# The fifth row block of x^T phi(k) by seven 64-column products, right ahead of KV

## The chip, the core and the metric

The kernel runs on one core of a Trainium2 chip. The metric is the time of one execution on the device in microseconds (us); the kernel before takes 182.53 us, the median of 3 runs from 182.36 to 182.84.

## What is computed

x is 2048 x 640 in bf16, and two linear-attention blocks A and B with their own weights read the same x. For each of them, with H = 32 heads of 20 columns:

```python
qkv = (x @ wqkv).reshape(B, S, 3, H, Dh)          # q, k, v
phi = lambda t: where(t > 0, t + 1, exp(t)) + 1e-6
pq, pk = phi(q), phi(k)
kv  = einsum("bhsd,bhse->bhde", pk, v)            # per head, 20 x 20
z   = einsum("bhsd->bhd", pk)
num = einsum("bhqd,bhde->bhqe", pq, kv)
den = einsum("bhqd,bhd->bhq", pq, z) + 1e-6
block = (num / den) @ wo
```

The output is g·A(x) + (1 − g)·B(x), where g = sigmoid((x · gate_w) summed over the columns), one number for each row.

## The kernel before

No v is ever computed. As kv = phi(k)^T x wv, the kernel makes G = x^T phi(k) (640 x 640, in two halves of 320 columns, `GT[0]` and `GT[1]`, called lo and hi here) and then KV = G^T wv for each head's group of columns. KV is folded into wo (M = KV·wo, 640 x 640), so that the last stage is (phi(q)/den)·M for A and B together.

**Order of the work.** The whole program is a hand-written order; each engine works through its own list in that order, and waits on semaphores where its data or its buffer isn't ready. The stages are: k and q of A (16 row chunks, then column units), A's G stage (`g_all(0)`), k of B (16 chunks of ten 320-column products, `k_chunk`, L227) with A's KV and M in between, q of B in ten units (`q_pass`), B's G stage, and then the pairs (`Pair`, L600), which make the output rows two blocks at a time with shared partial products. phi of a chunk is an exp on ScalarE (L205), a clamp on VectorE (L210) and a maximum on VectorE: either straight from the bank (L214) or, for a "lifted" chunk, from a copy with 1 added that ScalarE makes (L209, then L212).

**The G stage.** G is 5 row blocks of 128. `g_pass` (L307) makes the fifth one, columns 512 to 640 of x, by 32 products of 320 columns (`g_mm`, L328); in its course `z_pass` (L438) makes the sums of phi(k) from rows that VectorE added before (`z_sum`, `z_half`, `z_last`), and `zsel` from them. The other four blocks are made by `g_strassen` (L375): a 2 x 2 scheme with seven products on blocks of x (256 columns by 1024 rows) and of phi(k) (320 columns by 1024 rows), each of 16 matmuls (`g_prod`, L366). Its sums of x are `x_sum(1)` to `x_sum(4)` (SX1 to SX4, L334), those of phi(k) `k_sum(b, 1)` to `k_sum(b, 4)` (TK, L345), all on VectorE through `add_rows` (L546). The partial products lie in two PSUM slots called even and odd and are added on VectorE (L387, L435) with copies p1, u2 and u3 in SBUF.

Inside this stage stands den (`rec_pass`, L516; `by_group`, L172): 40 products of 256 columns by 32 rows of output, four side by side on the array. Behind it `rec(h)` on VectorE multiplies by the gate's factor (d, L525), takes the reciprocal (L530) and sends the result through DRAM (`r_store`, `r_load`) to R, by which `scale` (L576, L579) multiplies phi(q) in place.

**KV and M.** `kv_mm` (L457) takes six groups of columns times five row blocks, two tiles of 60 or 40 rows side by side: 60 products. `kv_mask` cuts the heads out. For A it stands behind k chunk 1 of B (`kv_a`, L480), for B behind the first pair's p1. `m_a` (L505) folds A's wo in between the later k chunks, `m_b` (L784) B's at the start of the pairs, with the copies from PSUM shared by ScalarE and VectorE (L791) and a round trip through DRAM (`m_store`, `m_load`). `load_wo` brings wo into a buffer with the tag "wo".

**Sums for the pairs.** `p_diff` (L550) and `p_sums` (L555) make differences and sums of phi(q) of A and B in four parts of 256 columns on VectorE; part 0 of one of them is given to GpSimd (L799). `m_sum` makes those of M; `TM[0]` of A's M is made in B's G stage.

**Queues.** SyncE (SP) issues most DMAs in program order; ScalarE issues some of r_load, the load of wq for B and a few stores.

Of the kernel before, what the change touches and what calls it, by code (L numbers as in the profile page):

```python
# [24 lines left out]
NW = 6  # L25
# [7 lines left out]
def kernel(  # L33
# [21 lines left out]
    psum = banks.enter_context(tc.tile_pool(name="psum", bufs=1, space=bass.MemoryType.PSUM))  # L55

    turn = [0]

    def ps_raw(name, slot=None):

        if slot is None:
            slot = turn[0]
            turn[0] = (slot + 1) % 4
        return psum.tile([P, 4 * HB], BF16, tag=f"ps{slot}", name=name)
# [9 lines left out]
    GT2 = persist.tile([P, 2 * DT, HF], BF16, name="GT")  # L74
    GT = [GT2[:, n * DT:(n + 1) * DT, :] for n in range(2)]
# [19 lines left out]
    SX[4] = flat(M[1], "p c d -> p (c d)", ic)  # L95
    TK = [{k: flat(pqT[1], "p c s -> p (c s)", HF, k - 1) for k in (1, 2, 3, 4)}, {}]
# [4 lines left out]
    early = persist.tile([P, hc * HF], BF16, name="TM0")  # L101
    TM = [early[:, 0:DT * HF].rearrange("p (c n) -> p c n", c=DT)] + [None] * 3
    TK[1][2] = early[:].rearrange("p (i n) -> p i n", i=hc)
# [60 lines left out]
    for n in (HB,) * 6 + (HB // 2,):  # L164
        nc.tensor.matmul(warm[:, 1, 0:n], lhsT=one_l, rhs=one_r[:, 0:n], start=True, stop=True)
# [141 lines left out]
    def g_pass(b, c, slot):  # L307

        pt = ps(f"g{'AB'[b]}", slot)
        for i in range(ST):  # L310
            if b == 0 and i == 4:
                gate_exp()
            if i == (8 if b else 13):
                zsel = z_pass(b)
                if b:
                    p_diff(part[0])
                else:
                    x_sum(2)
                    gate_done(0)
            if b == 1 and i == 13:  # L320
                p_diff(part[1])
            for hf in range(2):
                g_mm(c, i, hf, pt)
        for hf in range(2):
            nc.scalar.copy(out=GT[hf][:, c, :], in_=pt[:, hf, 0:HF])
        return zsel

    def g_mm(c, i, hf, pt):  # L328
        nc.tensor.matmul(  # L329
            pt[:, hf, 0:HF], lhsT=xn[:, i, c * P:(c + 1) * P], rhs=pk[:, i, hf * HF:(hf + 1) * HF],  # L330
            start=(i == 0), stop=(i == ST - 1),
        )

    def x_sum(k, cuts=(0, hc)):  # L334

        x11, x21 = [xn[:, 0:hc, n:n + ic] for n in (0, ic)]
        x12, x22 = [xn[:, hc:ST, n:n + ic] for n in (0, ic)]
        a, b, op = {
            1: (x21, x22, ALU.subtract), 2: (x11, SX[1], ALU.subtract),
            3: (x21, x11, ALU.subtract), 4: (x12, SX[2], ALU.subtract),  # L340
        }[k]
        for lo, hi in zip(cuts, cuts[1:]):
            add_rows(SX[k][:, lo:hi], a[:, lo:hi], b[:, lo:hi], op)
# [21 lines left out]

    def g_prod(pt, left, right, first, lo=0, hi=hc):  # L366

        for i in range(lo, hi):
            for n in range(2):
                nc.tensor.matmul(  # L370
                    pt[:, n, 0:HF], lhsT=left[:, i, n * P:(n + 1) * P], rhs=right[:, i, :],
                    start=(first and i == 0), stop=(i == hc - 1), skip_group_check=not first,
                )

    def g_strassen(b, den):  # L375

        x11, x12 = [xn[:, k:k + hc, 0:ic] for k in (0, hc)]
        x22 = xn[:, hc:ST, ic:2 * ic]
# [4 lines left out]
        def temp(name):  # L383
            return work.tile([P, 2, HF], FP32, tag="osb", name=name, bufs=3)

        def add(dst, pt, sb):
            nc.vector.tensor_tensor(out=dst, in0=pt[:, :, 0:HF], in1=sb[:], op=ALU.add)  # L387

        even, odd = ps("gs0", 0), ps("gs1", 1)
        g_prod(even, x11, b11, True, 0, 1 - b)  # L390
        rec = den()
        rec(0)
        g_prod(even, x11, b11, True, 1 - b)
        p1 = temp("p1")
        nc.scalar.copy(out=p1[:], in_=even[:, :, 0:HF])
        if b == 0:
            x_sum(3)
        else:
            rec(1)
        g_prod(odd, SX[2], TK[b][2], True)  # L400
        u2 = temp("u2")
        add(u2[:], odd, p1)
        if b == 0:
            x_sum(4)
        else:
            p_diff(part[2])
            p_diff(part[3])
            m_sum(0)
        g_prod(even, x12, b21, False)
        nc.scalar.copy(out=lo[:, 0:2, :], in_=even[:, :, 0:HF])  # L410
        if b == 0:
            rec(1)
        r_load(b, 1, nc.scalar)
        if b == 0:
            wq[1] = load_w(1, "q", nc.scalar)
        scale(b, 0, 2, 0)
        g_prod(odd, SX[3], TK[b][3], False)
        u3 = temp("u3")
        add(u3[:], odd, p1)
        scale(b, 2, 4, 0)  # L420
        even = ps("gs0", 0)
        g_prod(even, SX[1], TK[b][1], True)
        if b == 1:
            load_wo(1, nc.sync)
        add(hi[:, 2:4, :], even, u3)
        scale(*((b, 0, 2, 1) if b else (b, 4, 5, 0)))
        g_prod(odd, x22, TK[b][4], False)
        if b == 1:
            scale(1, 4, 5, 0)
        add(lo[:, 2:4, :], odd, p1)  # L430
        if b == 1:
            scale(1, 2, 4, 1)
        g_prod(even, SX[4], b22, False)
        for n in range(2):
            nc.vector.tensor_tensor(out=hi[:, n, :], in0=even[:, n, 0:HF], in1=u2[:, n], op=ALU.add)  # L435
        if b == 0:
            scale(0, 0, 2, 1)
    def z_pass(b):  # L438

        dst = ps(f"z{'AB'[b]}", 1 - b)[:, 0, 0:DT * H]  # L440
# [16 lines left out]
    def kv_mm(b, dst):  # L457

        for k in range(NW):
            for i, c in enumerate((4, 2, 3, 0, 1)):  # L460
                for p0, hf, d0, w in kv_groups(k):
                    nc.tensor.matmul(
                        dst[p0:p0 + w, k * WT[0]:k * WT[0] + w], lhsT=wv[b][:, c, hf * HF + d0:hf * HF + d0 + w],
                        rhs=GT[hf][:, c, d0:d0 + w], start=(i == 0), stop=(i == DT - 1), tile_position=(0, p0),
                    )

# [12 lines left out]

    def kv_a():  # L480

        pt = ps("kvA")
        kv_mm(0, pt[:, 0])
        kv_mask(pt[:, 0])
# [31 lines left out]
    def rec_pass(b, zsel, slot):  # L516
# [5 lines left out]
        def rec(h):  # L522
# [8 lines left out]
            eng = nc.scalar if h else nc.sync  # L531
# [33 lines left out]

    def m_sum(k):

        lo, hi = slice(0, HF), slice(HF, D)
        a, b = M[0], M[1]
        left, right = {  # L570
            0: (a[:, :, hi], a[:, :, lo]), 1: (b[:, :, hi], TM[0]),
# [14 lines left out]
    def prod(dst, left, right, i, first):  # L586

        r0 = i * P
        for c in range(DT):
            nc.tensor.matmul(  # L590
                dst, lhsT=left[:, c, r0:r0 + P], rhs=right[:, c, :], start=(first and c == 0), stop=(c == DT - 1), skip_group_check=not first,
# [4 lines left out]

    def tmp(name, tag):
        return work.tile([P, HF], FP32, tag=tag, name=name)

    class Pair:  # L600

        def __init__(self, i):
            self.i = i
            self.last = i == ST // 2 - 1
            self.p1s, self.p15 = [xn[:, k * hc + i, :].bitcast(FP32) for k in range(2)]

        def store(self, k, lo=0, hi=D):
            eng = nc.scalar if self.last and (k or lo > HF) else nc.sync
# [36 lines left out]
        def p6(self):  # L645
            prod(self.at("x"), xT[:, :, 0:SH], TM[1], self.i, True)
            self.u6 = tmp("u6", "ex")
            nc.scalar.copy(out=self.u6[:], in_=self.at("x"))  # L648

        def u25(self):  # L650
            self.v = tmp("v", "zr")
            out_add(self.v[:], self.u6[:], self.p15)
# [23 lines left out]
    def load_w(b, which, eng, cuts=(0, DT)):  # L676
        lo = {"q": 0, "k": D, "v": 2 * D}[which]
        t = wpool.tile([P, DT, D], BF16, tag="w" + which, name=f"w{which}{'AB'[b]}")
# [3 lines left out]

    def load_wo(b, eng):
        t = wo_sb[b] = wpool.tile([P, NW, D], BF16, tag="wo", name=f"wo{'AB'[b]}")
# [28 lines left out]
    def g_all(b):  # L713

        zsel = g_pass(b, DT - 1, 2 - b)
        g_strassen(b, lambda: rec_pass(b, zsel, 3 - b))


# [3 lines left out]
    for n in range(2):  # L722
        for i in range(CB if n else 0, CB * 2 * n):
            k_chunk(0, i, lifted=i % 2 == 0)
        for m in (0, 2):
# [4 lines left out]
    wv[0] = load_w(0, "v", nc.sync)  # L730
    load_wo(0, nc.sync)
    wk[1] = load_w(1, "k", nc.sync)

# [6 lines left out]
    with tc.manual_schedule():  # L740
        for i in range(hc + 1, ST):
# [3 lines left out]
            if i == hc + 3:  # L745
                k_sum(0, 1)
# [4 lines left out]
        g_all(0)  # L751

        turn[0] = 3
        for i in range(ST):
            k_chunk(1, i, lifted=i in (5, 7, 9, 13))
            if i in (3, 5, 7):
                scale(0, i // 2 + 1, i // 2 + 2, 1)
            if i > 3 and i % 2 == 0:
                m_a(i // 2 - 2)
            if i == 1:  # L760
                kv_a()
                wv[1] = load_w(1, "v", nc.sync)
# [6 lines left out]
        g_all(1)  # L769
# [8 lines left out]
        with late_pool("mid") as mid:  # L778
# [15 lines left out]
            pairs[0].p1()  # L794
            scale(1, 4, 5, 1)
            kv = acc["z"][1]
            kv_mm(1, kv)
            kv_mask(kv)
            p_sums(slice(0, 2 * P), (1,), nc.gpsimd)  # L799
            pairs[1].p1()  # L800
# [92 lines left out]
```

## Time and profile before

| | |
|---|---|
| median of 3 runs | 182.53 us (182.36 to 182.84) |
| the profiled execution | 182.66 us |
| its span in the profile | 180.9 us (1.76 us lie outside) |
| granted TensorE clock | 1.000 |

In the profile PE is TensorE's products, PEld its weight loads, DVE VectorE, ACT ScalarE, POOL GpSimd and SP SyncE. The page's first part gives busy time, share of the span and number of instructions of each engine. A row of the chain of waits, in order of time, gives start, length, and what stood on the path. A row of a timeline gives start, length, engine, line, operation, the tiles (out<-in), their shapes, and in brackets the idle time of the engine ahead of it and what ended it. A row of the groups by line gives engine, operation, tiles, shapes and count, then the busy time in us, the mean of one in ns, and the idle time ahead. All starts count from the span's start.

### The profile page before, as it was taken

To read this page: it belongs to the slowest core of one execution; us is meant where nothing else is said; L and a number is where in the kernel's file an instruction comes from. 1 tells how busy PE (TensorE), PEld (TensorE's weight loads), DVE (VectorE), ACT (ScalarE), POOL (GpSimd) and SP (SyncE) were. 2 spreads that over 40 slices of the span, in tenths; PEclk is the share of its full clock that TensorE was granted. 3 is DMA by queue.
4 is the path that set the end of the run, shared out by engine and by line. 5 is a ranking of instruction groups with operands and counts; after the bars stand their busy time and mean duration, and the time that the engine had idled before them with its cause. 6 is when DMAs were issued, how large, how long until landed. Compare 5 with 4: busy or idle time off the path is not lost.

```text
span 180.9 us, 3415 instructions
## 1 busy us (share of the span) xinstructions
PE 176.8 (98%) x1340; PEld 119.3 (66%) x1345; DVE 147.6 (82%) x247; ACT 85.8 (47%) x140; POOL 5.4 (3%) x18
## 2 busy tenths in 40 slices
PE   8999999999999999999999999999999999999993
PEld 4565657765577777777775555577777777777772
DVE  0386868989999896888778999969999799977863
ACT  2245846889972101378784779931101763111010
POOL 6000000000000000000000000000002300000000
PEclk9999999999999999999999999999999999999999
DMA  5999999524100217331115000000325451133323
GB/s 183 214 261 170 240 364 297 110 38 145 58 0 5 72 32 226 91 127 35 57 34 186 23 0 0 0 0 18 112 79 144 129 179 60 36 109 112 109 92 127
DMA packets 22842, 19.33 MB, mean 107 GB/s; under 512 B 10538, under 2 KB 22058, under 8 KB 22826
## 3 DMA queue, kind: packets, MB, share of 16 engines
q1 hardware_dynamic: 20744, 16.95, 34.0%
q10 hardware_dynamic: 2082, 2.17, 3.7%
q8 instruction: 10, 0.16, 0.4%
q14 instruction: 6, 0.05, 0.1%
HBM read 12.29 MB, written 4.53 MB: 93 GB/s over the span
## 4 chain that ended last, share of the span: by engine, by line
PE 95%; DMA 2%; issue 0%; DVE 0%; ACTq 0%
PE gs L370 17%; PE kA L218 12%; PE ox L590 12%; PE kB L218 12%; PE qB L281 12%; PE qA L281 6%; PE oz L590 6%; PE qA L291 5%; PE gA L329 2%; PE gB L329 2%; DMA wkA<-in_A_wqkv_dram 2%; PE ow L590 2%; PE qA L301 1%; PE mA L494 1%; PE s L494 1%; PE oy L590 1%
## 5 line engine op out<-in xcount | busy, mean ns | idle before, releaser
L218 PEld LDWEIGHTS <-xT 128*128 128x128 bf16 x320 | 31.0, 98 | 13.1 <-DVE xT L243 0.8
L210 DVE TENSOR_SCALAR e<-e 128x640 bf16<-128x640 bf16 (+2 forms) x53 | 18.9, 357 | 7.2 <-ACT e L205 6.6
L218 PE MATMUL kA<-wkA,xT 128*128 128x320 bf16 (+1 forms) x160 | 22.8, 300 | 0.3 <-DMA wkA<-in_A_wqkv_dram 0.3
L218 PE MATMUL kB<-wkB,xT 128*128 128x320 bf16 x160 | 23.1, 299 | 0.0
L281 PE MATMUL qB<-xT,wqB 128*128 128x512 bf16 x98 | 21.6, 379 | 0.1
L205 ACT ACTIVATE e<-kB 128x640 bf16<-128x640 f32 x16 | 11.3, 704 | 15.8 <-DMA wqB<-in_B_wqkv_dram 9.4
L281 PEld LDWEIGHTS <-wqB 128*128 128x128 bf16 x100 | 11.7, 117 | 9.7
L205 ACT ACTIVATE e<-kA 128x640 bf16<-128x640 f32 x16 | 11.2, 705 | 8.4 <-PE kA L218 8.4
L205 ACT ACTIVATE e<-qA 128x1024 bf16<-128x1024 f32 (+1 forms) x11 | 10.4, 946 | 6.4 <-PE qA L291 5.1
L648 ACT COPY u<-ox 128x320 f32<-128x320 f32 x8 | 3.4, 426 | 20.4 <-PE ox L590 20.4
L205 ACT ACTIVATE e<-qB 128x1024 bf16<-128x1024 f32 x10 | 10.2, 1024 | 5.6 <-PE qB L281 4.9
L370 PEld LDWEIGHTS <-xn 128*128 128x128 bf16 x96 | 9.2, 98 | 3.9 <-issue 0.4
L370 PEld LDWEIGHTS <-S 128*128 128x128 bf16 x96 | 9.4, 98 | 3.6
L281 PE MATMUL qA<-xT,wqA 128*128 128x512 bf16 x49 | 10.9, 379 | 0.1
L214 DVE SCALAR_TENSOR_TENSOR pk<-kB,e 128x640 bf16<-128x640 f32 x12 | 9.9, 825 | 1.3
L590 PEld LDWEIGHTS <-xT 128*128 128x128 bf16 x85 | 8.1, 98 | 2.9
L590 PEld LDWEIGHTS <-pqTB 128*128 128x128 bf16 x80 | 7.8, 98 | 3.2
L590 PEld LDWEIGHTS <-pqTA 128*128 128x128 bf16 x80 | 7.7, 98 | 2.9
L370 PE MATMUL gs<-pk,xn 128*128 128x320 bf16 x64 | 9.5, 299 | 0.0
L281 PEld LDWEIGHTS <-wqA 128*128 128x128 bf16 x50 | 5.9, 117 | 4.8
L291 PE MATMUL qA<-xT,wqA 128*128 128x512 bf16 x38 | 8.9, 379 | 0.1
L212 DVE TENSOR_TENSOR pk<-pk,e 128x640 bf16<-128x640 bf16 x12 | 5.9, 492 | 2.8 <-ACT pk L209 2.2
(123 smaller groups left out, 297.1 us busy)
## 6 DMA issues: line engine op xcount, KB each, us to landing
xn<-in_A_x_dram SPq DMA_DIRECT2D x1, 2240.0 KB, 9.7
out_dram<-pk SPq DMA_DIRECT2D x14, 160.0 KB, 1.8
wvA<-in_A_wqkv_dram SPq DMA_DIRECT2D x1, 800.0 KB
wkB<-in_B_wqkv_dram SPq DMA_DIRECT2D x1, 800.0 KB, 4.6
wqB<-in_B_wqkv_dram ACTq DMA_DIRECT2D x1, 800.0 KB, 5.0
wvB<-in_B_wqkv_dram SPq DMA_DIRECT2D x1, 800.0 KB
MA<-mA_dram SPq DMA_DIRECT2D x1, 800.0 KB, 5.5
MB<-mB_dram SPq DMA_DIRECT2D x1, 800.0 KB
```

The lines of the kernel that those rows point to most:

```text
L205: nc.scalar.activation(out=e[:], in_=src, func=ACT.Exp)
L210: nc.vector.tensor_scalar(e[:], e[:], 1.0, EPS, op0=ALU.min, op1=ALU.add)
L212: nc.vector.tensor_tensor(out=dst, in0=dst, in1=e[:], op=ALU.max)
L214: nc.vector.scalar_tensor_tensor(out=dst, in0=src, scalar=1.0 + EPS, in1=e[:], op0=ALU.add, op1=ALU.max)
L218: nc.tensor.matmul(pt[:, hf, 0:w], lhsT=xT[:, c, i * P:(i + 1) * P], rhs=wk[b][:, c, hf * HF:hf * HF + w], start=(c == 0), stop=(c == DT - 1),
L281: nc.tensor.matmul(pt[:, u, :], lhsT=mixed(wq[b][:, c, :], m), rhs=xT[:, c, n * HB:(n + 1) * HB], start=(c == 0), stop=(c == DT - 1),)
L291: nc.tensor.matmul(pt[:, u, :], lhsT=mixed(wq[b][:, c, :], m + u), rhs=xT[:, c, n * HB:(n + 1) * HB], start=(c == 0), stop=(c == DT - 1),)
L329: nc.tensor.matmul(pt[:, hf, 0:HF], lhsT=xn[:, i, c * P:(c + 1) * P], rhs=pk[:, i, hf * HF:(hf + 1) * HF], start=(i == 0), stop=(i == ST - 1),
L370: nc.tensor.matmul(pt[:, n, 0:HF], lhsT=left[:, i, n * P:(n + 1) * P], rhs=right[:, i, :], start=(first and i == 0), stop=(i == hc - 1), s ...
L494: nc.tensor.matmul(dst[:w, 0:HF], lhsT=KVA[:rows, k, 0:w], rhs=wo_sb[b][:rows, k, n * HF:(n + 1) * HF], start=True, stop=True,)
L590: nc.tensor.matmul(dst, lhsT=left[:, c, r0:r0 + P], rhs=right[:, c, :], start=(first and c == 0), stop=(c == DT - 1), skip_group_check=not ...
L648: nc.scalar.copy(out=self.u6[:], in_=self.at("x"))
```

## The change

`g_pass`, `g_strassen`, `kv_mm` and `kv_a` go. A single `g_all(b, single)` makes the whole stage:

- The fifth row block is made by the same seven-product scheme on blocks of 64 columns of x. Each such product (`narrow`) is eight matmuls of 64 output rows by 320 columns, two side by side: one for the first half of the row chunks on partitions 0 to 63, one for the second half on 64 to 127. The two halves are never added to one another; GT gets a sixth row block per half, and wv's last 128 rows are loaded as two blocks of 64, each of them twice, on either half of the partitions (`load_narrow`, two DMAs on SP per input). KV has six row blocks in place of five, so 72 products.
- The narrow sums of x (`narrow_sums`, four of 512 columns) are made once, on VectorE, where `k_sum(0, 1)` stood; `k_sum(0, 1)` moves ahead of the second half of q A's first blocks. The one sum u6 + p15 of the narrow products is given to GpSimd.
- KV follows right behind, in the stage itself, for A and for B, step by step (`kv_step`) as its row blocks come in.
- The products of the wide scheme stand in another order, and den, `x_sum(3)`, `x_sum(4)`, u2, u3 and `rec(1)` with them: in A, den comes behind half of x12·b21, then SX2, SX3, x22 and SX4. The even and odd slots become four single PSUM banks, each half of a sum by itself.
- A's ten scales of 1024 columns all stand in k B's loop, nine chunks of it are lifted (before: four), and `p_diff` of parts 2 and 3 stands behind its chunks 13 and 15.
- In B's stage `load_wo(1)` goes first, into the buffer with the tag "wq"; the scales of B's second half stand in the stage, those of the first half behind `m_b`; `TM[0]` is made in two buffers of the exp's ring (`m_first`).
- Among the pairs, `p_sums` of part 0 is back on VectorE between `m_b`'s copies, and the later `p_sums` are spread over five iterations. The stores of pairs 1 to 4 are one DMA for both row blocks. The warm-up is 13 products of 256 columns in place of 6 of 512 and one of 256.

The core of the diff:

```diff
-    GT2 = persist.tile([P, 2 * DT, HF], BF16, name="GT")
+    GT2 = persist.tile([P, 2 * (DT + 1), HF], BF16, name="GT")
+    def narrow_sums():
+        for k in (1, 2, 3, 4):
+            x_sum(k, f0=2 * ic, w=P // 2, dst=SN)
...
+        for n in prod(even, x11, b11, True):
+            nc.scalar.copy(out=p1[:, n], in_=even[n])
+        at = 0 if b else 5
+        g_prod(third, SX[1], t[1], True, 0, at)
+        zsel = z_pass(b, 3)
+        if b == 0:
+            x_sum(2)
+            gate_done(0)
+        else:
+            p_diff(part[0])
+            p_diff(part[1])
+            g_prod(third, SX[1], t[1], True, 0, 4)
+            at = 4
+            rec = rec_pass(1, zsel, 3)
+            rec(0)
+            rec(1)
+        g_prod(third, SX[1], t[1], True, at)
+        if b == 0:
+            g_half(even[0], x12, b21, 0, False)
+            rec = rec_pass(0, zsel, 3)
+            rec(0)
+            x_sum(3)
+            g_half(even[1], x12, b21, 1, False)
+        else:
+            for n in prod(even, x12, b21, False):
+                pass
...
+        for n in prod(odd, SX[2], t[2], True):
+            add(u2[:, n], odd[n], p1[:, n])
+            if b:
+                m_first(3 * n, 3 - n)
+        if b == 0:
+            x_sum(4, 0, hc // 2)
+        u3 = g_temp("u3")
+        for n in prod(odd, SX[3], t[3], False):
+            add(u3[:, n], odd[n], p1[:, n])
+            if n == 0 and b == 0:
+                x_sum(4, hc // 2, hc)
...
+        def narrow(pt, left, right, first):
+            for i in range(hc // 2):
+                for r in range(2):
+                    rows = slice(r * P // 2, (r + 1) * P // 2)
+                    j = r * hc // 2 + i
+                    nc.tensor.matmul(
+                        pt[rows, :], lhsT=left[:, j, :], rhs=right[:, j, :], start=(first and i == 0),
+                        stop=(i == hc // 2 - 1), tile_position=(0, rows.start), skip_group_check=not first,
+                    )
...
+        narrow(A, x11, b11, True)
+        nc.scalar.copy(out=p1, in_=A)
+        narrow(B, SN[2], t[2], True)
+        nc.scalar.copy(out=u6, in_=B)
+        C, G = two("o")
+        narrow(C, x12, b21, True)
+        add(lo[:, DT - 1, :], C, p1)
+        if b:
+            scale(1, 4, 5, 1)
+        narrow(A, SN[1], t[1], False)
+        nc.scalar.copy(out=p15, in_=A)
+        narrow(B, SN[3], t[3], False)
+        add(hi[:, DT, :], B, p15)
+        narrow(G, SN[4], b22, True)
+        add(v, u6, p15, nc.gpsimd)
+        add(hi[:, DT - 1, :], G, v)
+        kv = single("e", 0) if b else ps("kvA", 2)[:, 0]
+        wide = range(DT - 1)
+        kv_step(b, kv, (0, 1), wide, True)
+        narrow(B, x22, t[4], False)
+        add(lo[:, DT, :], B, p1)
+        kv_step(b, kv, (2, 3, 4, 5), wide)
+        kv_step(b, kv, (0, 1, 2), (DT - 1,))
+        kv_step(b, kv, (3, 4, 5), (DT - 1, DT))
+        kv_step(b, kv, (0, 1, 2), (DT,))
+        kv_mask(kv)
...
-            k_chunk(1, i, lifted=i in (5, 7, 9, 13))
-            if i in (3, 5, 7):
-                scale(0, i // 2 + 1, i // 2 + 2, 1)
+            k_chunk(1, i, lifted=i in (1, 2, 3, 5, 7, 9, 11, 13, 15))
+            if i in (13, 15):
+                p_diff(part[(i - 9) // 2])
+            if i in scales:
+                c, h = scales[i]
+                scale(0, c, c + 1, h)
```

More of the change, by code (lines that the diff above doesn't have):

```diff
@@ L364, in z_last, with g_half @@
         add_rows(Z[:, 0, 0:HF], Z[:, 0, 0:HF], Z[:, 0, HF:D], ALU.add)
+    def g_half(pt, left, right, n, first, lo=0, hi=hc):
+        for i in range(lo, hi):
+            nc.tensor.matmul(
+                pt, lhsT=left[:, i, n * P:(n + 1) * P], rhs=right[:, i, :],
+                start=(first and i == 0), stop=(i == hc - 1), skip_group_check=not first,
+            )
     def g_prod(pt, left, right, first, lo=0, hi=hc):
@@ L373, in g_prod, with g_temp, k_blocks @@
                 )
-    def g_strassen(b, den):
-        x11, x12 = [xn[:, k:k + hc, 0:ic] for k in (0, hc)]
-        x22 = xn[:, hc:ST, ic:2 * ic]
+    def g_temp(name):
+        return work.tile([P, 2, HF], FP32, tag="osb", name=name, bufs=3)
+    def k_blocks():
         b11 = pk[:, 0:hc, 0:HF]
         b21, b22 = [pk[:, hc:ST, n * HF:(n + 1) * HF] for n in range(2)]
-        lo, hi = GT
[L383 to L395, printed above, removed]
-        if b == 0:
+        return b11, b21, b22
@@ new lines, in g_all, with two, prod, add @@
+    def g_all(b, single):
+        x11, x12, _, x22 = x_blocks(0, ic)
+        b11, b21, b22 = k_blocks()
+        t = TK[b]
+        lo, hi = GT
+        def two(name):
+            return [single(name, n)[:, 0:HF] for n in range(2)]
+        def prod(pts, left, right, first, lo=0, hi=hc):
+            for n in range(2):
+                g_half(pts[n], left, right, n, first, lo, hi)
+                yield n
+        def add(dst, a, b, eng=nc.vector):
+            eng.tensor_tensor(out=dst, in0=a, in1=b, op=ALU.add)
+        odd, even = two("o"), two("e")
+        third = ps("gs2", 2)
+        p1 = g_temp("p1")
+        if b == 0:
+            gate_exp()
+        else:
+            load_wo(1, nc.sync)
+        for n in prod(even, x11, b11, True):
[19 more added lines that the diff above has]
+            rec(0)
@@ L397, in g_strassen @@
             x_sum(3)
+            g_half(even[1], x12, b21, 1, False)
         else:
[L399 to L402, printed above, removed]
+            for n in prod(even, x12, b21, False):
+                pass
+        for n in range(2):
+            nc.scalar.copy(out=lo[:, n, :], in_=even[n])
         if b == 0:
-            x_sum(4)
+            wq[1] = load_w(1, "q", nc.scalar)
         else:
-            p_diff(part[2])
-            p_diff(part[3])
-            m_sum(0)
@@ L409, in g_strassen @@
-        g_prod(even, x12, b21, False)
-        nc.scalar.copy(out=lo[:, 0:2, :], in_=even[:, :, 0:HF])
+            r_load(1, 1, nc.scalar)
+        u2 = g_temp("u2")
+        for n in prod(odd, SX[2], t[2], True):
[9 more added lines that the diff above has]
+                x_sum(4, hc // 2, hc)
@@ L411, in g_strassen @@
+        for n in range(2):
+            add(hi[:, 2 + n], third[:, n, 0:HF], u3[:, n])
+        for n in prod(odd, x22, t[4], False):
+            add(lo[:, 2 + n], odd[n], p1[:, n])
+            if b and n == 0:
+                scale(1, 0, 2, 1)
         if b == 0:
             rec(1)
[L413 to L419, printed above, removed]
@@ L564, in p_sums, with m_first, column @@
                 add_rows(dst, a, b, op, eng)
+    tm_first = []
+    def m_first(lo, n):
+        t = work.tile([P, n, HF], BF16, tag="e", name="TM0", bufs=3)
+        add_rows(t[:], M[0][:, lo:lo + n, HF:D], M[0][:, lo:lo + n, 0:HF], ALU.subtract)
+        TM[0] += [t[:, c, :] for c in range(n)]
+        tm_first.append((lo, t))
+    def column(right, c):
+        return right[c] if isinstance(right, list) else right[:, c, :]
     def m_sum(k):
@@ L590, in prod @@
             nc.tensor.matmul(
-                dst, lhsT=left[:, c, r0:r0 + P], rhs=right[:, c, :], start=(first and c == 0), stop=(c == DT - 1), skip_group_check=not first,
+                dst, lhsT=left[:, c, r0:r0 + P], rhs=column(right, c), start=(first and c == 0), stop=(c == DT - 1), skip_group_check=not first,
             )
@@ L824 @@
             pairs[i].p5()
-        for n in range(3):
-            p_sums(part[n], (2, 4))
+        p_sums(part[0], (2, 4))
+        p_sums(part[1], (2,))
         inner = ctx.enter_context(late_pool("inner"))
@@ L857 @@
             if i in later:
-                p_sums(part[3], (later[i],))
+                n, k = later[i]
+                p_sums(part[n], (k,))
         after.p7()
```

212 lines of the change are left out of this document (103 added, 109 removed).

## The prediction

> **What bounds the kernel now.** I read the page's head first, then TensorE's own waits, then the chain in order of time, then VectorE's timeline at the places that the diff touches.
>
> ```profile
> span 180.9 us, 3415 instructions
> PE 176.8 (98%) x1340; PEld 119.3 (66%) x1345; DVE 147.6 (82%) x247; ACT 85.8 (47%) x140; POOL 5.4 (3%) x18
> ```
> ```profile
> PE xt L165 <- PEq L877: 0.8, 1, 0.8
> PE kA L218 <- DMA wkA<-in_A_wqkv_dram: 0.3, 1, 0.3
> ```
>
> TensorE (PE) is busy 98% of the span. Its waits have two rows only, both at the start. So the time is TensorE's work; whatever shortens that work shortens the kernel, and any new wait of TensorE is paid in full, as nothing else is on the chain. VectorE (DVE) is 82% busy, so a reordering of its work can make such waits.
>
> ```profile
> 49.17 3.53 PE gA L329 x26
> 52.70 0.17 PE zA L442 x5
> 52.88 0.82 PE gA L329 x6
> 53.70 0.27 PE gs L370 x2
> 53.98 1.21 PE denA L177 x40
> 55.18 15.05 PE gs L370 x110
> 70.23 2.72 PE kB L218 x20
> 72.94 0.96 PE kvA L462 x60
> ...
> 116.27 2.17 PE gB L329 x16
> 118.44 0.17 PE zB L442 x5
> 118.62 2.18 PE gB L329 x16
> 120.80 1.21 PE denB L177 x40
> ```
> ```profile
> 122.06 0.42 DVE L525 SCALAR_TENSOR_TENSOR d<-denB,geB 128x256 f32<-128x256 f32 x1 [1.29 <-PE denB L177]
> ```
>
> These are the stages that change (start, length, what; the last row, of VectorE's timeline, is used below). A product of 320 columns costs 2.72/20 = **0.136 us**, here p; the fifth row block is 32 of them for A (3.53 + 0.82 = 4.35 us) and 32 for B (2.17 + 2.18 = 4.35 us), and the whole sits on the path.
>
> **The change, part by part.**
>
> *Fifth block.* 64 products go, 64p = 8.70 us. In their place stand seven narrow products per input, each of eight matmuls, two side by side: 112 matmuls in 56 pairs. No row of before has a pair of 64 columns over 320. If a pair runs side by side it costs p, 7.62 us in all; one after the other, 2p, 15.2 us. The nearest row is denA: 40 products of 256 columns, four side by side, in 1.21 us, so 0.121 per group of four, where 256 columns alone would be 0.8p = 0.109; ten groups leave 0.12, which I take as the price of entering and leaving such a mode. That mode is entered as often after as before (den and KV, where the narrow products join KV), so I take p per pair: −64p + 56p = **−1.09 us**.
>
> ```profile
> 53.90 0.99 PEld L177 LDWEIGHTS <-zsel 128*32 128x32 bf16 x40 [0.26 <-DVE zsel L446]
> L462 PEld LDWEIGHTS <-wvA 128*60 128x60 bf16 x40 | 0.8, 109 | 0.3 <-issue 0.3
> ```
>
> The 40 loads of den took 0.99 us beside their products, so loads of side-by-side tiles are hidden there. The Trainium skill, "TensorE: Matmul & The Clock Gate", Part 3 ("What overlaps and what doesn't"), speaks against this change: a load overlaps products in flight only where its row group differs, and the tiles here differ by column. By it each pair would pay a load, 56 × 0.109 = 6.1 us; the den row does not bear it out, and it is a rival below.
>
> *KV.* Six steps in place of five: 24 products more, (0.96 − 0.12)/60 = 0.014 us each, **+0.34 us**. Where KV stands costs nothing in itself.
>
> *A's stage, VectorE.* Now VectorE's chain of den must fit under fewer products.
>
> ```profile
> 53.40 0.32 DVE L446 TENSOR_TENSOR zsel<-zA,headE 128x160 bf16<-128x160 f32 x1
> ...
> 55.29 0.43 DVE L525 SCALAR_TENSOR_TENSOR d<-denA,geA 128x256 f32<-128x256 f32 x1
> 55.75 1.75 DVE L530 RECIPROCAL rT<-d 128x256 bf16<-128x256 f32 x1
> 57.42 1.16 DVE L546 TENSOR_TENSOR S<-xn 128x2048 bf16<-128x2048 bf16 x1
> 59.47 0.82 DVE L387 TENSOR_TENSOR u<-gs,p 128x640 f32<-128x640 f32 x1 [0.89 <-PE gs L370]
> ```
> ```profile
> L595 DVE TENSOR_TENSOR v<-u,xn 128x320 f32<-128x320 f32 x8 | 3.9, 490 | 3.2 <-ACT u L648 3.2
> L648 ACT COPY u<-ox 128x320 f32<-128x320 f32 x8 | 3.4, 426 | 20.4 <-PE ox L590 20.4
> L546 POOL TENSOR_TENSOR pqTA<-pqTA,pqTB 128x1280 bf16<-128x1280 bf16 x1 | 2.6, 2603 | 135.5 <-PE oz L462 135.5
> ```
>
> Before, 46 products lay between den and the product that reads x_sum(3) (14 of x11·b11, 16 each of SX2 and x12·b21): 46p = 6.3 us, and VectorE sat idle 0.89 us. After, 24 lie there (half of x12·b21, all of SX2): 1.21 + 24p = 4.47 us from den's start. VectorE, in its order: d at 55.29 − 53.98 = 1.31, x_sum(3) at 57.42 − 53.98 = 3.44, to 4.60; the first half of u2 behind it, 320 wide, 0.49 us, begun 0.08 before the end of its predecessor (as 57.42 stands to 55.75 + 1.75) and over at 5.01; TensorE's load 0.18 later (53.72, zsel's end, to 53.90): 5.19. SX3's product needs both, its bank by u2 and its weights by x_sum(3). TensorE waits 5.19 − 4.47 = **+0.72 us**. Bounds: 0.1 if d starts when the first half of den is done (0.6 earlier), 1.2 if u2 takes its full 0.82.
>
> *Both tails.* The last sum of the fifth block, B + p1, feeds KV's last six products; beside it lie 50 KV products, 0.70 us. From bank to VectorE is 0.21 us (59.47 against the end of the 30 products behind den, 55.18 + 30p = 59.26), the sum 0.49, the load 0.18: 0.88, so **+0.18 us**, twice: +0.36. The sum u6 + p15 goes to GpSimd; for 320 float32 columns no row exists. Bounds are VectorE's 0.49 and the whole 2.60 of GpSimd's 1280 bf16 columns; I take a quarter of that, 0.65, since the columns are a quarter. From the first narrow product on: the fourth ends at 2.18, its copy on ScalarE at 2.18 + 0.21 + 0.43 = 2.82, GpSimd at 3.5, VectorE's sum G + v behind it at 4.0 and TensorE's load at 4.2; that sum is first read after six products (3.26), 16 KV products (0.22), the last narrow one (0.54) and 38 more of KV (0.53), at 4.56. So at 0.65 it is in time by 0.35 us. VectorE's last sum is in line behind it: at 1.3 both come later and a stage loses about 0.6 more, at 2.6 about 1.9.
>
> *k B's loop.*
>
> ```profile
> L210 DVE TENSOR_SCALAR e<-e 128x640 bf16<-128x640 bf16 x32 | 10.3, 323 | 4.3 <-ACT e L205 3.7
> L214 DVE SCALAR_TENSOR_TENSOR pk<-kB,e 128x640 bf16<-128x640 f32 x12 | 9.9, 825 | 1.3
> L212 DVE TENSOR_TENSOR pk<-pk,e 128x640 bf16<-128x640 bf16 x12 | 5.9, 492 | 2.8 <-ACT pk L209 2.2
> L579 DVE TENSOR_TENSOR pqTA<-pqTA,R 128x1024 bf16<-128x1024 bf16 x4 | 2.7, 684 | 0.0
> 72.36 0.33 DVE L210 TENSOR_SCALAR e<-e 128x640 bf16<-128x640 bf16 x1
> ```
>
> The loop takes in seven more scales and the two p_diffs, and nine chunks instead of four take their shift on ScalarE, at 0.323 + 0.492 in place of 0.323 + 0.825 us of VectorE. A chunk of 10 products is 10p = 1.36 us of TensorE. With overlaps a plain chunk with a scale is 1.18 + 0.60 = 1.78, a shifted one 0.83 + 0.60 = 1.43. So VectorE falls behind over the first six chunks, all with scales: from 2.13 (72.36 − 70.23) past the loop's start it comes to 12.9, where TensorE wants the bank at 9 chunks and two small pairs, 12.8. **+0.1**; bounds 0 and 0.7, half a chunk. What VectorE still lags at the loop's end, q B's ten units take up, but for what z's sums show.
>
> *B's z and m_b.*
>
> ```profile
> 116.87 0.84 DVE L546 TENSOR_TENSOR GT<-GT 128x640 bf16<-128x640 bf16 x2
> ...
> 141.97 0.88 DVE L791 CAST pk<-s 80x320 bf16<-80x320 f32 x2 [0.34 <-PE s L494]
> ...
> 144.11 2.30 DVE L546 TENSOR_TENSOR pqTA<-pqTA,pqTB 128x1280 bf16<-128x1280 bf16 x3
> ```
>
> z's sums ended at 117.71, its product started at 118.44: 0.7 of margin, and the lag that the loop leaves may eat it: **+0.1** (0 to 0.7). p_sums of part 0 (a third of the 2.30 us for three alike) now stands between m_b's casts where VectorE idled 0.34 us: **+0.1** (0 to 0.4).
>
> ```profile
> 25.34 0.43 DVE L210 TENSOR_SCALAR e<-e 128x1024 bf16<-128x1024 bf16 x1 [1.19 <-ACT e L205]
> ```
>
> *At no cost:* k_sum(0,1), 2560 columns or 1.16 × 2560/2048 = 1.45 us, moves into q A's first half, where VectorE idled 1.19 us; the remaining 0.3 delays a clamp whose bank is not wanted for a whole unit. The four narrow sums (four of 512 columns, a quarter of 57.42's 2048 each, some 1.4 us with starts) take its place; without that room they would be late for nothing before A's tail, 20 us on. On SP's queue, load_wo for B moves ahead of B's stage, the second copy of wv's last rows and rec(1) of A follow; each has a stage's length, 15 us, before its reader. The merged stores take away issues. Three p_sums (2.30) and B's five scales left for the pairs (5 × 0.68) stand before p2, 5.7 us; the cover is 50 products of p1 and p5, 6.8 us. Without it, each late scale would cost its 0.7 us once.
>
> **The sum.** −1.09 + 0.34 + 0.72 + 0.36 + 0.1 + 0.1 + 0.1 = **+0.63 us**. The span goes from 180.9 to 181.5, the profiled execution from its 182.66 (1.76 outside the span) to 183.29. That execution lies 0.13 above the median of the runs, 182.53; on the median the forecast is 182.53 + 0.63 = **183.2 us**.
>
> **Rivals.** (1) *A's VectorE chain fits.* Its place is den to u2; it decides at 4.47 us from den's start. If d needs only den's first half, 0.6 us earlier, 0.1 is left of the 0.72: 182.5. If the tails and the three small terms are covered as well, the gain of 0.75 stands whole: 181.8. For it: in A no idle time stands ahead of d, so its row doesn't show what released it. Against: in B, VectorE stood idle and d still began at 122.06, when the whole den was over (120.80 + 1.21), and x_sum(3) is in line ahead of u2. (2) *GpSimd's sum is slow.* At 1.3 us, twice what I took, each tail loses 0.6 more: 183.2 + 1.2 = 184.4 (at the whole 2.60, 187.0). For it: 2.60 us for one sum, the only such row. Against: a quarter of the columns. (3) *The change doesn't do what it says:* the pairs run one after another (+56p = 7.6: 190.8) or pay their loads (+6.1: 189.3, the page's rule). Against: den's row.
>
> **How the numbers follow.** This kernel's time is told from no change beyond about 0.3%, 0.55 us. Forecast with its own range 182.8 to 183.7: 0.52, of which 0.33 lies above 183.08 and 0.19 within. 182.5, A's wait nearly gone: 0.24, of which 0.04 below 181.98. 181.8, all covered: 0.13. GpSimd slow: 0.08. No side-by-side gain: 0.03. Faster 0.04 + 0.13 = 0.17; same 0.19 + 0.20 = 0.39; slower 0.33 + 0.08 + 0.03 = 0.44. The range 182.0 to 184.4 leaves out the 0.13 below, the 0.03 and half of the 0.08, 0.2 in all; it takes in the bounds of the stall (0.1 to 1.2) and of GpSimd up to 1.3.
>
> **What would show it.** Narrow products in chain rows at 0.54 us for eight matmuls (right), 1.1 (rival 3). Of TensorE's waits, SX3's product on VectorE, about 0.7, once; KV's last products on VectorE's last sum, 0.2, twice; a wait on GpSimd's sum would be rival 2. KV of 72 products near 1.1. The forecast is wrong if TensorE's wait list stays at two rows, or if VectorE's lag shows in q B or B's z at over half a microsecond.

## The result, and the profile after

The changed kernel takes **183.29 us**, the median of 22 runs (182.91 to 185.62), against 182.57 us for 22 runs of the kernel before beside them: a ratio of 1.0047, 95% interval 1.0025 to 1.0069. It is slower, by 0.7 us; the forecast was 183.2. Its profiled execution has a span of 181.5 us at a granted clock of 1.0. The head of its page, and all of TensorE's waits of more than a moment (total in us, times, longest):

```profile
span 181.5 us, 3629 instructions
PE 177.5 (98%) x1423; PEld 121.0 (67%) x1423; DVE 151.1 (83%) x275; ACT 90.4 (50%) x151; POOL 4.5 (2%) x19
```
```profile
PE xt L174 <- PEq L973: 0.8, 1, 0.8
PE o L357 <- DVE u L396: 0.4, 1, 0.4
```

One wait is new, SX3's product on VectorE's u2 (L396, the add of u2 and u3), once: the place that the prediction named. In the chain of waits, in order of time, A's stage and the places where a row is longer than its like:

```profile
49.05 2.17 PE e L357 x16
...
54.67 1.23 PE denA L186 x40
55.90 0.02 issue
55.92 0.44 DVE d L592
...
59.13 0.49 DVE u L396
59.62 0.04 issue
59.66 4.51 PE o L357 x32
64.17 2.17 PE gs L366 x16
66.34 1.21 PE e L474 x16
67.55 0.54 PE o L474 x8
68.09 1.09 PE e L474 x16
69.18 0.54 PE o L474 x8
69.72 0.24 PE kvA L515 x16
69.96 0.60 PE e L474 x8
70.56 0.86 PE kvA L515 x37
71.42 6.90 PE kB L227 x50
...
84.30 0.37 PE mA L561 x2
...
95.01 21.58 PE qB L290 x100
116.59 2.17 PE e L357 x16
118.77 0.28 PE zB L525 x5
...
138.49 1.46 PE ox L673 x10
...
142.40 0.75 PE s L561 x4
...
165.64 2.08 PE ox L673 x15
```

What the reader is to see. Behind den the path runs through VectorE, where before it was TensorE without a break: d at 55.92, then the reciprocal and x_sum(3), u2 at 59.13, and SX3's product at 59.66. The narrow products (L474) stand at 0.54 us for eight matmuls and 1.09 for sixteen, 0.136 per pair. Four rows are longer than their like: mA at 84.30 (the others 0.27), zB (0.17 before), the third group of s at 142.40 (the others 0.55), and, by 0.04, six of the seven groups of fifteen products in the pairs (before, four of these six were at 2.04 and two at 2.06). The rows of before for these places, and the starts of before that the table below uses:

```profile
84.08 0.28 PE mA L494 x2
...
94.69 0.22 PE qB L281
...
137.32 0.68 PE ox L590 x5
...
142.88 0.55 PE s L494 x4
...
165.19 2.04 PE ox L590 x15
```

Stage by stage, from the starts in these rows and in those of before (KV counted with the stage that makes it):

| | before | after | change |
|---|---|---|---|
| to the G stage of A | 49.17 | 49.05 | −0.12 |
| G stage of A with KV | 21.06 + 0.96 | 71.42 − 49.05 = 22.37 | +0.35 |
| k of B, without A's KV | 24.46 − 0.96 | 95.01 − 71.42 = 23.59 | +0.09 |
| q of B | 21.58 | 21.58 | 0 |
| G stage of B with KV | 21.05 + 0.96 | 138.49 − 116.59 = 21.90 | −0.11 |
| pairs to the end, without KV | 180.9 − 137.32 − 0.96 = 42.62 | 181.5 − 138.49 = 43.01 | +0.39 |

The two G stages tell the tale: with the same saving in both, B's is shorter by 0.11 and A's longer by 0.35. The first row can't be put down to the change: in eight profiles of kernels that are the same up to there (the changed kernel and seven edits of it) A's G stage began anywhere between 48.56 and 49.15 us.

### The profile page after: what moved, and what is told of

Its sections match the earlier page's. It is cut to its first block, busy times and chain, and to the rows that moved or that the text cites. A ratio compares the mean times of both kernels' runs of the same rounds, so it can differ in the third digit from the quotient of the medians.

```text
span 181.5 us, 3629 instructions
## 1 busy us (share of the span) xinstructions
PE 177.5 (98%) x1423; PEld 121.0 (67%) x1423; DVE 151.1 (83%) x275; ACT 90.4 (50%) x151; POOL 4.5 (2%) x19
## 4 chain that ended last, share of the span: by engine, by line
PE 96%; DVE 2%; issue 1%
PE kA L227 12%; PE ox L673 12%; PE kB L227 12%; PE qB L290 12%; PE o L357 6%; PE qA L290 6%; PE oz L673 6%; PE gs L366 5%; PE qA L300 5%; PE e L357 4%; PE e L474 3%; PE ow L673 2%; PE xt L174 2%; PE o L474 1%; PE qA L310 1%; PE s L561 1%
## 5 line engine op out<-in xcount | busy, mean ns | idle before, releaser
L227 PEld LDWEIGHTS <-xT 128*128 128x128 bf16 x320 | 31.1, 98 | 12.9 <-DVE xT L252 0.4
L214 ACT ACTIVATE e<-qB 128x1024 bf16<-128x1024 f32 x10 | 10.2, 1024 | 4.9 <-PE qB L290 4.2
L221 DVE TENSOR_TENSOR pk<-pk,e 128x640 bf16<-128x640 bf16 x17 | 8.4, 493 | 2.9 <-ACT pk L218 1.6
L357 PE MATMUL e<-pk,xn 128*128 128x320 bf16 x64 | 9.5, 299 | 0.0
L484 ACT COPY pn<-e 128x320 f32<-128x320 f32 x2 | 0.9, 428 | 16.3 <-PE e L474 16.3
L678 DVE TENSOR_TENSOR pk<-ox,xn 128x320 bf16<-128x320 f32 x16 | 7.8, 485 | 0.7 <-PE ox L673 0.7
```

The costliest lines, as they stand in the source:

```text
L214: nc.scalar.activation(out=e[:], in_=src, func=ACT.Exp)
L221: nc.vector.tensor_tensor(out=dst, in0=dst, in1=e[:], op=ALU.max)
L227: nc.tensor.matmul(pt[:, hf, 0:w], lhsT=xT[:, c, i * P:(i + 1) * P], rhs=wk[b][:, c, hf * HF:hf * HF + w], start=(c == 0), stop=(c == DT - 1),
L357: nc.tensor.matmul(pt, lhsT=left[:, i, n * P:(n + 1) * P], rhs=right[:, i, :], start=(first and i == 0), stop=(i == hc - 1), skip_group_ch ...
L678: nc.vector.tensor_tensor(out=dst, in0=acc, in1=sb, op=ALU.add)
```

## The experiments

All are the changed kernel with one or more edits; times are medians, and each ratio is to the kernel before on the same chip, with its 95% interval. "A single run" is one time and one profile.

**x_sum(3) ahead of den's chain.**

```diff
+            x_sum(3)
             rec = rec_pass(0, zsel, 3)
             rec(0)
-            x_sum(3)
```

> x_sum(3) stands ahead of den's d and reciprocal on VectorE in A's stage; all else is the changed kernel. Theory (TensorE's 0.59 us wait ahead of SX3's first product is VectorE's row d, reciprocal, x_sum(3), u2): the 1.16 us of x_sum(3) fill the 0.86 us in which VectorE waits for den, d starts about 0.3 later, u2's first half is over 0.9 earlier than now, and the wait goes: span 181.5 to 180.9, time 183.3 to 182.7, no wait of TensorE on u. Rival (the wait only moves on to the next sum of that stage, since VectorE's total work there is the same): a wait of 0.4 or more turns up within the next 50 products, and the time stays at 183.1 to 183.3.

182.55 us, ratio 0.9994 (0.9972 to 1.0017), span 180.8. VectorE's timeline at that place (start, length; idle time in brackets), the first row from the changed kernel, the others from this run:

```profile
55.92 0.42 DVE L592 SCALAR_TENSOR_TENSOR d<-denA,geA 128x256 f32<-128x256 f32 x1 [0.86 <-PE denA L186]
...
54.87 1.22 DVE L613 TENSOR_TENSOR S<-xn 128x2048 bf16<-128x2048 bf16 x1
56.00 0.42 DVE L592 SCALAR_TENSOR_TENSOR d<-denA,geA 128x256 f32<-128x256 f32 x1
56.45 1.75 DVE L597 RECIPROCAL rT<-d 128x256 bf16<-128x256 f32 x1
58.15 0.49 DVE L396 TENSOR_TENSOR u<-o,p 128x320 f32<-128x320 f32 x1
59.24 0.49 DVE L396 TENSOR_TENSOR u<-o,p 128x320 f32<-128x320 f32 x1 [0.59 <-PE o L357]
```

x_sum(3) fills the 0.86 us in which VectorE waited for den, u2's first half comes at 58.15 instead of 59.13, and now VectorE waits for TensorE. TensorE's list of waits has only its first row left. From den's row to SX4's products (gs) it took 64.17 − 54.67 = 9.50 us, and here 63.48 − 54.56 = 8.92: the wait was **0.58 us**, and nothing came up in its place. The list of waits has only 0.4 of it, as a row behind a wait begins with its first product, and one in an unbroken chain with its predecessor's end: in the changed kernel the 32 products of that row take 4.51 us, where 32p are 4.35.

**u6 and v in places of their own.**

```diff
-            u = g_temp("u")
-            self.u6, self.v = u[:, 0], u[:, 1]
+            self.u6, self.v = [
+                GT2[:, 2 * n:2 * n + 2, :].rearrange("p c n -> p (c n)").bitcast(FP32) for n in (self.i % 2, 2 + self.i % 2)
+            ]
```

> In the pairs, u6 and v get places of their own (in the space of GT, free by then) instead of the two halves of one buffer of a ring of three. Theory (p7 comes about 0.04 us late in most pairs because ScalarE's copy of u6 has a third wait, for its own earlier write in that ring): the pairs' three products in a row take 2.04 us as before, not 2.08, and the span falls by 0.15 to 0.2, to 181.3; time 183.1. Rival (p7 is late because VectorE's later p_sums hold up what p7 waits for): the rows stay at 2.08 and the time at 183.3.

182.93 us, ratio 1.0019 (1.0009 to 1.0029). The same group of fifteen products in the chain:

```profile
165.29 2.04 PE ox L673 x15
```

All six such groups from 159 us on are at 2.04 or 2.05 again, 0.2 us together; one row of five products, at 154.36, went from 0.68 to 0.73, so the pairs gain 0.15. In the changed kernel u6's copy on ScalarE waits on three semaphores in these groups (TensorE, VectorE, and ScalarE's own earlier write in the ring), here on two. The rows of the copy's line show where the wait for TensorE stands, in the changed kernel and here (instruction, count, shortest, median and longest in ns):

```profile
L736 ACTq EVENT_SEMAPHORE  x8: 17/2691/3393, 151.3 to 172.6; - x8
...
L737 ACTq EVENT_SEMAPHORE  x8: 17/17/17, 153.7 to 172.1; - x8
```

With three, an instruction of its own ahead of the copy does the waiting; with two, the copy itself does, and it starts some 0.04 us sooner (0.88 us behind p6's first product in place of 0.92). p7, which adds to the bank that the copy reads, has just the five products of p4 between for cover. VectorE's p_sums, the rival, stand where they stood. The median fell by 0.36, 0.2 more than the rows account for; where that comes from is open.

**The fifth block at full width, at the narrow products' place.**

```diff
-        narrow(A, x11, b11, True)
...
-        kv_step(b, kv, (0, 1, 2), (DT,))
+        fifth = two("e")
+        for n in range(2):
+            for i in range(ST):
+                nc.tensor.matmul(
+                    fifth[n], lhsT=xn[:, i, 2 * ic:D], rhs=pk[:, i, n * HF:(n + 1) * HF],
+                    start=(i == 0), stop=(i == ST - 1),
+                )
+            nc.scalar.copy(out=GT[n][:, DT - 1, :], in_=fifth[n])
...
+        kv_step(b, kv, range(NW), wide, True)
+        kv_step(b, kv, range(NW), (DT - 1,))
```

> The fifth row block is made by 32 full-width products of 320 columns per input, at the place of the narrow products, without their sums; KV has 60 products in place of 72; everything else is the changed kernel's order. Theory (the narrow products themselves are worth 8 products of 0.136 us, less 24 KV products of 0.014 and some 0.15 of switches): 1.09 - 0.34 - 0.15 = 0.6 us slower than the changed kernel, 183.9, span 182.1, with A's wait of 0.59 still there. Rival (the narrow products are what makes the changed kernel slower): 182.6 or less.

184.08 us, ratio 1.0083 (1.0068 to 1.0098). From SX4's products (gs) to the next stage it takes 71.39 − 63.90 = 7.49 us, by these rows, where the changed kernel takes 71.42 − 64.17 = 7.25:

```profile
63.90 2.17 PE gs L366 x16
...
71.39 6.90 PE kB L227 x50
```

So a stage gains 0.24 us by its narrow products, 0.48 in all. The two kernels differ by 0.8 us by the medians and 0.66 by the ratios; most of the rest lies in the pairs, where m_b's first group of products took 0.73 in place of 0.55. The narrow products are not what makes the changed kernel slower.

**All five moves together.** As above, and three more:

```diff
-            p_sums(part[0], (1,))
+            p_sums(part[0], (1,), nc.gpsimd)
...
-        scales = {0: (0, 0), 1: (1, 0), 2: (2, 0), 3: (3, 0), 4: (4, 0), 5: (0, 1), 7: (1, 1), 9: (2, 1), 10: (3, 1), 11: (4, 1)}
+        scales = {0: (0, 0), 1: (1, 0), 2: (2, 0), 3: (3, 0), 5: (4, 0), 7: (0, 1), 9: (1, 1), 10: (2, 1), 11: (3, 1), 12: (4, 1)}
...
-        at = 0 if b else 5
+        at = 1 if b else 5
...
-            g_prod(third, SX[1], t[1], True, 0, 4)
+            g_prod(third, SX[1], t[1], True, at, 4)
```

> The changed kernel with five small moves: x_sum(3) ahead of d in A; one scale fewer in the first six chunks of k B (and one more behind chunk 12); B's z product two products later; part 0 of p_sums on GpSimd; u6 and v in places of their own. Theory (the losses are the waits counted one by one: 0.59 + 0.10 + 0.11 + 0.21 + 0.2): 1.2 us under the changed kernel, span 180.3, time 182.1, 0.5 under the kernel before. Rival (taking the waits away lets others come up behind them): less than half of it, 182.7 or more.

**182.07 us, ratio 0.9973 (0.9961 to 0.9984), faster than both kernels**; span 180.4. TensorE's list of waits has only its first row left, and in the chain the rows that answer to the long ones (mA, zB, s) are at their length:

```profile
83.79 0.27 PE mA L561 x2
...
118.42 0.17 PE zB L525 x5
...
141.68 0.55 PE s L561 x4
```

1.2 us under the changed kernel, as the sum of the single waits said. The last three moves were not run one by one; these rows are what shows them. In the runs with the first or the second move alone they stayed long (0.37, 0.28 and 0.75 in both).

**The same moves with the full-width block.** The edits of the last two experiments in one kernel.

> The full-width fifth block (32 products of 320 columns per input, KV of 60 products, no narrow sums) in the order of the changed kernel, with the five small moves that took its waits away. Theory (the moved order is worth nothing by itself, and what the freed kernel gains on the kernel before is the narrow products' net 0.5): 182.6, the same as the kernel before, and 0.5 over the kernel with the five moves and the narrow products. Rival (the gain of that kernel comes from its order, not from the narrow products): 182.1.

182.95 us, ratio 1.0012 (1.0001 to 1.0023): 0.9 us over the kernel with narrow products by the medians, 0.7 by the ratios. So the moved order by itself is worth nothing, or costs 0.2, and the narrow products carry the whole gain, somewhat more than expected; about 0.25 of it lies in each G stage (7.49 against 7.24 from SX4's products on), and another 0.18 in m_b's late start, which this kernel has too.

**The two halves in turn instead of side by side.**

```diff
-            for i in range(hc // 2):
-                for r in range(2):
+            for r in range(2):
+                for i in range(hc // 2):
```

> The changed kernel with the eight matmuls of each narrow product in another order: first the four of the lower half of the partitions, then the four of the upper half, so that hardly a pair of neighbours lies on different halves. Theory (a pair costs one product, 0.136 us, because its two tiles run side by side): 42 of the 56 pairs come apart at least, 3 of 4 in each product, 42 x 0.136 = 5.7 us, up to 56 x 0.136 = 7.6: span 187.2 to 189.1, and rows of 16 narrow matmuls 1.9 to 2.2 us long in place of 1.09. Rival (a narrow matmul of 64 rows is cheap by itself, or a pair pays its loads either way): span 181.5 to 182, rows of 1.1 to 1.2.

A single run, 182.83 us, span 181.1; the theory missed:

```profile
67.08 0.54 PE o L474 x8
```

The row is the same though four matmuls of one half are now issued before the first of the other. Either two tiles still run beside one another, or a matmul of 64 output rows is cheap wherever it lies. The next run tells these apart.

**Seven of eight matmuls on one half.**

```diff
-                    rows = slice(r * P // 2, (r + 1) * P // 2)
+                    q = r if i == 0 else 0
+                    rows = slice(q * P // 2, (q + 1) * P // 2)
...
```

> The changed kernel with seven of the eight matmuls of each narrow product on the lower half of the partitions and one on the upper half (the result is the same, since KV adds the halves). It asks what the run with the halves in turn left open: whether two narrow matmuls share the time of one because they lie on different halves, in whatever order they are issued, or because a matmul of 64 output rows is cheap. Theory (the halves run side by side, and TensorE starts a matmul for a free half ahead of those that wait for the other): seven in a row on one half, 7 x 0.136 = 0.95 us per product in place of 0.54, 14 x 0.41 = 5.7 us more, span 187.2, rows of 16 narrow matmuls 1.9 us. Rival (a matmul of 64 rows takes half the time wherever it lies): span 181.5 as before, rows of 1.1.

A single run, 188.9 us, span 187.2, as the theory had it.

```profile
66.44 1.75 PE e L475 x14
68.19 0.03 PE o L475
68.22 0.24 PE e L475 x2
68.46 0.68 PE o L475 x5
```

On one half each matmul takes its 0.136 us (five in 0.68). At 68.19 a matmul of the third product (o) starts ahead of two of the second (e) that stand before it in the program: it is the one for the free half. TensorE's timeline has it start at 67.89, between matmuls of the second product (five from 67.35, two from 68.03), and these still follow one another at 0.136 us: it took no time from them.

**The last narrow product without cover.**

```diff
-        narrow(B, x22, t[4], False)
-        add(lo[:, DT, :], B, p1)
         kv_step(b, kv, (2, 3, 4, 5), wide)
         kv_step(b, kv, (0, 1, 2), (DT - 1,))
         kv_step(b, kv, (3, 4, 5), (DT - 1, DT))
+        narrow(B, x22, t[4], False)
+        add(lo[:, DT, :], B, p1)
```

> The changed kernel with the last narrow product moved behind the 50 KV products that stood after it, so that only its own sum lies between it and the six KV products that read it. The wait of TensorE shows the whole of bank to VectorE, sum, and VectorE to TensorE. Theory (a product that waits only for its moving operand starts about 0.04 us after VectorE's end, its weights being loaded ahead): 0.21 + 0.49 + 0.04 = 0.74 us per stage at most, span 182.8 to 182.9. Rival, as the prediction had it (0.18 us as for a weight load behind zsel): 0.88 per stage, span 183.1 to 183.2.

A single run, 185.18 us, span 183.5. The chain at the tail:

```profile
69.22 0.88 POOL un L396
...
70.67 0.32 PE kvA L515 x9
...
71.59 0.02 issue
71.61 0.50 DVE GT L396
72.11 0.04 issue
72.15 0.27 PE kvA L515 x5
```

From VectorE's end to TensorE's product it is 0.04 us, not 0.18; with the prediction's 0.21 from bank to VectorE (counted from the end of a product's slot, ahead of the modelled end in this row) the chain is 0.21 + 0.50 + 0.04 = 0.75. The 0.50 and the 0.04 are as the theory had them; the 0.21 is taken over, not measured here. The span is 0.6 over what the theory expected and 0.3 over the rival's, as taking the cover away also laid bare GpSimd's sum: it and VectorE's sum behind it, on the chain now, hold TensorE up by about 0.3 in each stage.

**GpSimd's sum on VectorE.**

```diff
-        add(v, u6, p15, nc.gpsimd)
+        add(v, u6, p15)
```

> The changed kernel with the one sum u6 + p15 of the narrow products on VectorE (0.49 us) in place of GpSimd (0.87). Theory (GpSimd's sum is in time; VectorE's two idle times of 0.3 us behind it lie off TensorE's path): the same within 0.1 us, span 181.4 to 181.6, 183.3. Rival of the prediction (GpSimd's sum is slow enough to hold up the tail): 0.1 to 0.6 us less per stage, 183.0 or under.

183.52 us, ratio 1.0042 (1.0017 to 1.0067), span 181.8: no gain. The span is 0.2 over the expectation. In each stage the last KV row is 0.93 where it was 0.86, as VectorE's last sum comes later, and one more of mA's rows in k of B is long (0.42). In the changed kernel GpSimd's sum is in time.

## Why the prediction was right, point by point

| step | predicted | measured |
|---|---|---|
| fifth block and KV, with both tails | −1.09 + 0.34 + 0.36 = −0.39 | 2 × (5.08 − 5.31) = −0.46 |
| A: VectorE's chain under 4.47 us | +0.72 | +0.58 |
| k of B, behind its ninth chunk | +0.1 | 0.37 − 0.27 = +0.10 |
| B's z | +0.1 | 0.28 − 0.17 = +0.11 |
| m_b | +0.1 | 0.75 − 0.55 = +0.20 |
| pairs, u6 and p7 | 0 | +0.2 |
| sum | +0.63 | +0.73; +0.6 in the span, with the first row of the stages |

5.08 is 71.42 − 66.34, and 5.31 is 3.53 + 0.82 + 0.96 of before. **The first rival** (d needs only den's first half) fell: in the changed kernel d starts at 55.92, behind the whole of den at 55.90. A's wait itself, its place and its cause were right, and shown by the run that takes it away. Counted from den's row, the sum is over at 59.62 − 54.67 = 4.95 us (predicted 5.01) and the product starts at 4.99 (5.19), 0.04 behind the sum where the prediction had 0.18. The cover, 1.21 + 1.19 + 2.17 = 4.57 in the run without the wait, is 0.10 longer than its 4.47, as the eight products behind den take 1.19 and not 8p. That leaves 0.42, and the 0.16 that the list of waits doesn't have makes 0.58.

**The tails were mis-sized.** The prediction's "the load 0.18" is the time from zsel's end on VectorE to den's first weight load. That row tells of something else. These two, of before and of the changed kernel, show the same idle time of 0.26 us ahead of a first load whose data had long been ready:

```profile
120.73 0.99 PEld L177 LDWEIGHTS <-zsel 128*32 128x32 bf16 x40 [0.26 <-issue]
...
66.27 0.28 PEld L474 LDWEIGHTS <-xn 128*64 128x64 bf16 x6 [0.26 <-issue]
```

In the first, zsel had been ready since 118.98 + 0.32 = 119.30; the second has no zsel. So the row tells what it costs to go from full-width products to tiles, and not how long a load waits behind VectorE. The run without cover shows 0.04 from VectorE's sum to KV's product; of a chain of 0.21 + 0.49 + 0.04 = 0.74 under a cover of 0.70 some 0.04 is left, not 0.18. (Whether it would be longer if the sum were loaded as weights, and were not the moving operand, is not shown.) What the tails didn't cost came back elsewhere: a stage takes 5.08 us where 28 pairs (3.81), 72 KV products at 0.014 (1.01) and the 0.12 of entering make 4.94. The narrow products take 1.21 + 0.54 + 1.09 + 0.54 + 0.60 = 3.98 of it. Of their 0.17 over 28 pairs, 0.12 is the entering, and 0.06 the product behind KV, on a bank that VectorE's sum had only just read (69.29 + 0.49 = 69.78, against its start at 69.84); the rest is KV, at 1.10. The two errors nearly cancel, which is luck.

**k of B and z.** Place and cause fit: in the run with all five moves, which takes one scale out of the first six chunks and sets z two products later, both rows are at their length. The sizes fit by luck. The 12.9 us of k of B do not come out of the prediction's own times: 2.13, six chunks with scales (2 × 1.78 + 4 × 1.43) and the seventh without (1.18) make 12.6, under the 12.8 at which the bank is wanted; measured, VectorE's last row of the seventh chunk ended at 83.36 + 0.82 − 71.42 = 12.76. For z the 0.1 was a choice within 0 to 0.7.

**GpSimd** took 0.87 us for its sum, more than the 0.65 of the estimate and less than the 1.3 from which rival 2 counted; VectorE's sum behind it still came in time.

**The pairs were missed.** The prediction had no term for u6 and v moving into one ring; the six rows at 2.08 are shown to be that by the run which undoes it. m_b's term was right in kind and half the size: in VectorE's timeline the casts of two groups follow p_sums in one stretch (1.75 us from 141.92), where before each group's stood apart with 0.34 us idle ahead.

**The sum.** The terms were off by −0.07, −0.14, +0.10 and +0.2. That they add up to within 0.1 us of the forecast is luck in part; the largest loss, where it lies and what takes it away are not. The list of waits has two rows, as the prediction's sign of being wrong has it, but one of them is the wait that it forecast.

**Pairs side by side**: right at 0.136 us, so rival 3 fell. The loads of the narrow products (110 ns each) are hidden: sixteen matmuls with their loads stand in rows of 1.09. By the rule of the Trainium skill, "TensorE: Matmul & The Clock Gate", Part 3 ("What overlaps and what doesn't"), that a load overlaps products in flight only where its row group differs, it would have been 6.1 us more; the trace doesn't agree.

## What to carry to other kernels

A saving on a full engine is worth what is left after every wait that its reordering makes; list what the second busiest engine does in line between each pair of dependent products, and put work that depends on nothing into the time in which that engine waits for the first. Here one line moved was worth 0.6 us, about as much as what the narrow products bring (0.5 by the rows, 0.7 by the ratios). When a time is borrowed from a row, look whether that row was waiting for what you take it to show.

## What the runs showed of the hardware

Tiles on different column halves do not have to be issued in turn: with four matmuls of one half ahead of four of the other, eight still took 0.54 us, and with seven on one half TensorE ran a product's matmul for the free half before earlier ones for the busy half. The Trainium skill, "TensorE: Matmul & The Clock Gate", Part 3 ("What overlaps and what doesn't"), has matmuls start strictly in program order; these two runs do not agree with it. From full-width products to tiles, the first weight load began after 0.26 us without a load in three places (den in before at 53.90 and 120.73, the narrow products at 66.27), in the last two with its data long ready, and the first row of tiles was 0.12 us longer than its products alone (1.21 against 1.09). A short ScalarE copy began about 0.04 us later where the wait for TensorE stood on an instruction ahead of it than where the copy itself waited (2.08 against 2.04 us for fifteen products).
